# Batch 0 between the two stages of a Fourier mixing kernel: twelve on-chip copies in place of a trip through memory, another order of the first loads, and 60 starting products

## The chip, the cores and the metric

The kernel runs on one core of a Trainium2 chip. A core has a matrix engine (PE in the profile, with its weight loads as PEld), a vector engine (DVE), a scalar engine (ACT), GpSimd (POOL) and SyncE (SP), each with an instruction stream of its own that runs in order and waits on semaphores. SP, ACT and POOL issue transfers, and 16 DMA engines carry them out. SBUF is the on-chip memory of 128 partitions, PSUM the memory into which PE writes. The metric is the time of one execution on the device in microseconds (us), lower is better.

## The reference, cut to what matters

```python
# x: (8, 2496, 256)
X = np.fft.fft(np.fft.fft(x, axis=1), axis=2).real      # mixing over the sequence, then over the features
t = X.reshape(19968, 256)
logits = t @ w_gate                                      # 8 experts
e = argmax(logits, 1)
gate = softmax(logits)[e]
y = relu(t @ w1[e]) @ w2[e]                              # w1[e]: 256 x 1024, w2[e]: 1024 x 256
out = gate * y
```

Each of the 8 sequences ("batches") is transformed as a whole, and every one of its 2496 tokens then goes through one expert. Transforms and expert products are in float32.

## The kernel before, in words

The transform of a batch has two stages. **First stage** (`first`, L325): x of a batch comes in three thirds, `xq` (`load`, L284), each 112 partitions x 2048 floats, 896 KB, in three buffers. DVE folds a third (`fold`, L299; `fold_d`, L292), which uses the symmetry of the transform over positions and over features, and leaves four slices. PE multiplies each slice by a table of waves, `w1` (`half1`, L311), into PSUM tiles `s1`; ACT copies two slices at a time into `t1`. The third's four slices are written to a DRAM tensor `Td` of the batch (L342), and when all three are there, two transfers (`regroup`, L351) read it back as `t4`, in which the partition is another index of the transform: 120 values that belong together lie in 120 partitions, in 11 groups. For batches 0 and 1 ACT issues the writes, for the later ones SP. For each third of batch b > 0 that has been used, `load` asks for a third of batch b + 1.

**Second stage** (`second`, L361). `turn_last` (pr in the profile) mends one column of `t4`; `group` (p, from t and table) does the short transform of a group into `zz`; for each of ten windows of 128 rows PE does the transform over the features and the gate's logits at once (p, from zz and table), ACT copies what is left over, and DVE forms two sets of result rows (L410). After five windows `route` (L416) picks each row's expert and its place in a sorted list `Xs` in DRAM (rk are PE's running counts). Ten scatters per half then send the rows there: POOL issues them (`send`, L462). For batch 0 the places come from DVE as whole numbers; for later batches ACT and POOL turn them.

**Experts** (`experts`, L730). `plan` (L478) makes lists of blocks of 512, 256 or 128 rows of one expert. For each block SP reads an offset from such a list, then the rows (xb, `fetch_rows`) and the weights (w_sb, `fetch_weights`, 2 x 1 MB). DVE turns the rows (xT), PE does the product with w1 (ph), relu follows, PE does the product with w2 (py), and POOL scatters the rows into the output. Batch 0 has two blocks of 256 and four of 128.

**Order.** The order of instructions on each engine is the program's order, written out by hand: generators that are advanced in turns. `ahead_of(b)` (L930) is the first stage and the regrouping; `mixed(b)` (L936) advances the second stage of b together with the first stage of b + 1. The main part loads the constants, issues 16 products of ones (`WARM`), runs the first stage of batch 0 to its end, asks for x of batch 1 and for the regrouped values, prepares the gate's table (pg), takes seven steps of batch 1's first stage, and then runs the second stage of batch 0, with one step of batch 1 at every second step. Then expert work is taken step by step, with side work of the next batches at a rate that comes from the amount of work. Before the first block of all, nine turns of side work are taken (L784) between the request of its rows and the turning of its rows.

Of the kernel before, what the change touches and what calls it, by code (L numbers as in the profile page):

```python
# [12 lines left out]
F32 = mybir.dt.float32  # L13
# [8 lines left out]
NA, NB = 104, 24  # L22
# [10 lines left out]
HALF = -(-NG // 2)  # L33
LAST = NW * 128 - (NG - 1) * GP
NT = B * S
E, F = 8, 1024
# [149 lines left out]
AHEAD = 12  # L186
WARM = 16
MOST = max(k for now in rounds() for _, k, _ in now)
# [27 lines left out]
def kernel(ctx: ExitStack, tc, x, w_gate, w1, w2, out):  # L216
# [64 lines left out]
    ones = cp.tile([128, 128], BF16, name="ones16")  # L281
    waves = const_dram("w1", consts["w1"])

    def load(b, q):  # L284

        if b < B:
            xq = xp.tile([NP, 8, D], F32, tag="xq", name="xq", bufs=3)
            row = (b * NQ + q) * NA
            nc.sync.dma_start(out=xq[:].rearrange("p j d -> p (j d)"), in_=x[row:row + NP])
            ahead[b, q] = xq[0:NA]  # L290

    def fold_d(o, a, n):  # L292
# [30 lines left out]
    ahead = {}  # L323

    def first(b):  # L325

        pm0 = xp.tile([NA, D], F32, tag="pm0", name="pm0")
        for q in range(NQ + 1):
            f = iter(())
            if q < NQ:  # L330
                xq = ahead.pop((b, q))
                f = fold(xq, q, pm0[:])
            next(f, None)
            yield
            if q:
                t1 = xp.tile([NP, 4, D], F32, tag="t1", name="t1")
                half1(b, q - 1, 0, pm, pm0, t1)
            next(f, None)
            yield
            if q:  # L340
                half1(b, q - 1, 1, pm, pm0, t1)
                (nc.sync if b > 1 else act).dma_start(out=Td[b][:, 4 * (q - 1) * D:4 * q * D], in_=t1[:].rearrange("p j d -> p (j d)"))  # L342
                if b:
                    load(b + 1, q - 1)
            next(f, None)
            pm = xq[:, 4:8]
            yield
# [3 lines left out]
    def regroup(b, h):  # L351
        t4 = sp.tile([128, HALF, D], F32, tag="t4", name="t4")
        n = min(HALF, NG - h * HALF)
# [3 lines left out]
        ahead[b, "t4", h] = t4  # L357

    zz = cp.tile([128, 2, NW * 128], F32, name="zz")

# [369 lines left out]
    def experts(todo):  # L730
# [44 lines left out]
        for k, (b, size, last, at) in enumerate(todo):  # L775
            n, m = size // 128, BIG // size
            if not k:
# [5 lines left out]
                fetch_some(0)  # L783
                for _ in range(9):  # L784
                    yield 0, False
# [144 lines left out]
    def ahead_of(b):  # L930

        yield from first(b)
        regroup(b, 0)
        regroup(b, 1)

    def mixed(b):  # L936
# [12 lines left out]
    vec.memset(ones[:], 1.0)  # L949
    act.dma_start(out=con["w1"][:, 0:4], in_=waves[:, 0:4])  # L950
    load(0, 0)
    load(0, 1)
    nc.sync.dma_start(out=con["w1"][:, 4:], in_=waves[:, 4:])
    load(0, 2)
    nc.sync.dma_start(out=table[:], in_=const_dram("table", packed))
    nc.sync.dma_start(out=con["rt"][:], in_=const_dram("rt", consts["rt"]))
    nc.sync.dma_start(out=wg[:], in_=w_gate)
    for k in range(WARM):
# [122 lines left out]
```

## Time and profile before

| what | value |
|---|---|
| median of 3 runs | 1258.53 us (1257.82 to 1259.17) |
| the profiled execution's own time | 1258.56 us |
| its span, first to last instruction | 1256.8 us |
| mean granted PE clock | 0.976 |
| PE busy | 1208.1 us (96%) |
| DVE, ACT, POOL busy | 759.6, 431.3, 447.5 us |
| moved by DMA | 249.79 MB, mean 199 GB/s |
| first product of an expert (ph) starts | 89.55 us |

A row of the profile's timeline gives start and duration in us, engine, line, operation, what is written from what with shapes, the number of instructions in it, and in brackets the idle time of the engine before it and what ended it. In the names buffer numbers are left out, so that w stands for the table of waves, t for t1 and t4, p for the products of the second stage, w_sb for weights. A row of the waits gives the waiting instructions, what they waited for, the total in us, the number of waits and the longest. A row of the chain of work gives start, duration and what ran.

### The profile page before, as it was taken

To read this page: it belongs to the slowest core of one execution; us is meant where nothing else is said; L and a number is where in the kernel's file an instruction comes from. 1 tells how busy PE (TensorE), PEld (TensorE's weight loads), DVE (VectorE), ACT (ScalarE), POOL (GpSimd) and SP (SyncE) were. 2 spreads that over 40 slices of the span, in tenths; PEclk is the share of its full clock that TensorE was granted. 3 is DMA by queue.
4 is the path that set the end of the run, shared out by engine and by line. 5 is a ranking of instruction groups with operands and counts; after the bars stand their busy time and mean duration, and the time that the engine had idled before them with its cause. 6 is when DMAs were issued, how large, how long until landed. Compare 5 with 4: busy or idle time off the path is not lost.

```text
span 1256.8 us, 22295 instructions
## 1 busy us (share of the span) xinstructions
PE 1208.1 (96%) x7289; PEld 1076.3 (86%) x7289; DVE 759.6 (60%) x1804; ACT 431.3 (34%) x1167; POOL 447.5 (36%) x527
## 2 busy tenths in 40 slices
PE   5759999999999999999999999999999999999997
PEld 3648998777788899888988899889999999999996
DVE  3455434343456788566866578686888784444653
ACT  1424332333243433434343333442333332222222
POOL 0154527054117522472226603472364241111112
PEclk6869999999999999999999999999999999999998
DMA  8859899873548434673336435453347237878787
GB/s 235 261 174 350 308 317 311 221 237 122 154 153 263 151 110 163 184 234 116 102 124 211 138 96 162 138 180 101 106 139 206 94 105 284 277 285 284 280 292 284
DMA packets 163216, 249.79 MB, mean 199 GB/s; under 512 B 118601, under 2 KB 130227, under 8 KB 143516
## 3 DMA queue, kind: packets, MB, share of 16 engines
q1 hardware_dynamic: 146327, 203.28, 50.7%
q0 software_dynamic: 15888, 42.14, 9.1%
q10 hardware_dynamic: 885, 2.94, 0.7%
q8 instruction: 59, 0.97, 0.3%
q14 instruction: 57, 0.47, 0.1%
HBM read 194.91 MB, written 54.83 MB: 199 GB/s over the span
## 4 chain that ended last, share of the span: by engine, by line
PE 82%; DVE 9%; DMA 4%; ACT 2%; issue 2%; POOL 0%; SPq 0%; POOLq 0%; DVEq 0%; ACTq 0%
PE py L221 25%; PE ph L221 13%; PE a L221 11%; PE c L221 9%; PE p L221 6%; PE b L221 6%; PE d L221 5%; PE e L221 4%; PE s L221 3%; DMA xq<-in_x_dram 1%; DVE xT L584 1%; DMA Td<-t 1%; DVE y L684 1%; DMA Xs<-rows,pi 1%; DVE hT L639 1%
## 5 line engine op out<-in xcount | busy, mean ns | idle before, releaser
L236 POOL DMA_INDIRECT out_dram<-y,ro x163 | 161.4, 990 | 625.3 <-ACT y L680 301.3
L221 PE MATMUL py<-w_sb,hT 128*128 128x256 f32 x1504 | 339.5, 379 | 0.0
L221 PEld LDWEIGHTS py<-w_sb,hT 128*128 128x128 f32 x1504 | 281.4, 190 | 36.9 <-issue 1.0
L236 POOL DMA_INDIRECT Xs<-rows,pi x160 | 162.4, 1015 | 112.0 <-DVE rows L410 56.7
L221 PE MATMUL ph<-xT,w_sb 128*128 128x128 f32 (+2 forms) x992 | 171.1, 328 | 11.2 <-DVE xT L584 11.1
L221 PEld LDWEIGHTS ph<-xT,w_sb 128*128 128x128 f32 x992 | 136.3, 192 | 35.1 <-issue 16.8
L410 DVE SCALAR_TENSOR_TENSOR rows<-p,zs 128x129 f32<-128x129 f32 x160 | 48.9, 348 | 128.8 <-ACT lg L408 124.8
L221 PE MATMUL a<-xT,w_sb 128*128 128x256 f32 (+1 forms) x512 | 117.8, 357 | 0.0
L838 DVE TENSOR_SCALAR hT<-ph 128x512 f32<-128x512 f32 x43 | 29.7, 691 | 123.7 <-PE ph L221 63.7
L587 ACT ACTIVATE xT<-xT 128x256 f32<-128x256 f32 (+1 forms) x94 | 36.5, 388 | 179.2 <-DVE xT L584 140.8
L221 PEld LDWEIGHTS a<-xT,w_sb 128*128 128x128 f32 x512 | 88.6, 190 | 9.7
L892 ACT ACTIVATE y<-py,xb 128x256 f32<-128x256 f32 x94 | 44.6, 475 | 152.2 <-PE py L221 152.2
L636 DVE TENSOR_TENSOR hT<-hT,b 128x512 f32<-128x512 f32 x57 | 39.2, 688 | 75.7 <-PE b L221 50.0
L646 ACT ACTIVATE hT<-a 128x512 f32<-128x512 f32 x57 | 34.0, 597 | 134.1 <-PE a L221 131.1
L221 PE MATMUL s<-xq,w 104*112 104x256 f32 (+2 forms) x208 | 62.8, 425 | 16.3 <-DVE xq L297 12.1
L469 POOL CAST pi<-due 128x1 int32<-128x1 f32 x140 | 45.1, 322 | 65.5 <-ACT due L468 65.5
L221 PE MATMUL a<-w_sb,hT 128*128 128x128 f32 x528 | 66.0, 276 | 0.0
L221 PEld LDWEIGHTS a<-w_sb,hT 128*128 128x128 f32 x528 | 63.1, 192 | 0.7
L221 PEld LDWEIGHTS p<-table,t 120*128 120x128 f32 x352 | 53.6, 202 | 10.6 <-ACT t L372 2.8
L221 PE MATMUL c<-xT,ws 128*128 128x256 f32 (+1 forms) x256 | 60.3, 362 | 1.0 <-DVE hT L642 0.2
L221 PEld LDWEIGHTS s<-xq,w 104*112 104x112 f32 x208 | 38.5, 204 | 26.3 <-DVE xq L297 10.8
L584 DVE STREAM_TRANSPOSE xT<-xb 128x512 f32<-128x512 f32 (+1 forms) x91 | 56.2, 631 | 7.6 <-DMA xb<-Xs 7.6
(149 smaller groups left out, 2072.6 us busy)
## 6 DMA issues: line engine op xcount, KB each, us to landing
w_sb<-in_moe_w_dram SPq DMA_DIRECT2D x132, 1024.0 KB
xq<-in_x_dram SPq DMA_DIRECT2D x24, 896.0 KB
xb<-Xs SPq DMA_DIRECT2D x112, 128.0 KB
Td<-t SPq DMA_DIRECT2D x18, 448.0 KB
t<-Td SPq DMA_DIRECT2D x8, 768.0 KB
t<-Td SPq DMA_DIRECT2D x8, 640.0 KB
xb<-Xs SPq DMA_DIRECT2D x52, 64.0 KB
xb<-Xs SPq DMA_DIRECT2D x88, 32.0 KB
```

The lines of the kernel that those rows point to most:

```text
L221: nc.tensor.matmul(o, lhsT=lhsT, rhs=rhs, start=start, stop=stop, **kw)
L236: return unordered(pool.indirect_dma_start(out=dst, out_offset=bass.IndirectOffsetOnAxis(ap=idx, axis=0), in_=rows, in_offset=None, bounds ...
L410: vec.scalar_tensor_tensor(rows[:, k + m, 0:NY], p3[:, 0:NY], zs[:, 0:1], zs[:, 1:], op0=ALU.add, op1=op)
L469: pool.tensor_copy(idx, due[:])
L584: vec.transpose(free(xT[:], 256 * h, [32, n // 32], [BIG, 2], [1, 32]), free(xb, 512 * h, [64, n // 32], [1, 2], [2, 32]))
L587: act.activation(odd, odd, ACTF.Copy, scale=-1.0)
L636: vec.tensor_tensor(h12, h11, b[:], op=add)
L639: vec.tensor_tensor(h21, h12, d[:], op=add)
L646: act.activation(h11, a[:], ACTF.Relu)
L684: vec.tensor_tensor(o, o, p[:], op=add)
L838: vec.tensor_scalar(o, ph[:], 0.0, None, op0=ALU.max)
L892: act.activation(y[:, i % 2], py[:], ACTF.Copy, scale=meta[:, i, 1:2])
```

## The change

**Between the stages, batch 0 alone.** `first_whole` takes the place of `first(0)`. It folds and multiplies two slices at a time. Its table of waves, `wp`, has 110 columns in another order, so that after ACT's copy a slice lies in `t1` as 110 partitions, and one transfer inside SBUF per slice (12 in all: even slices by ACT, odd ones by SP) puts it where the second stage reads it: 10 partitions, 12 apart, x 11 groups x 256 floats. Td and the regrouping are not used for batch 0. `t4` is now one tile `t4s` for all batches, in two halves; before, each half came from a pool of two buffers. `natural` makes the table of waves for the other batches, `w1`, from `wp`, with three copies of DVE.

**Order of the first loads.** The waves come in three pieces (slices 0 to 3, 4 to 7, the rest), and the last third of x of batch 0 in two halves. `table`, `rt`, `wg`, the constants `bt` and the pad rows of `Xs` are now issued by POOL, behind a one-element copy that waits for the last piece of waves. x of batch 1 is asked for by SP inside `first_whole`: the first third after the eighth slice's copy, the other two after the twelfth. The last third of x of batch 2 is asked for after batch 1's regrouping.

**Turns.** 60 products of ones in place of 16. Three steps of batch 1's first stage stand before batch 0's second stage in place of seven, and the interleaving begins at the second stage's step 4. Twelve turns of side work stand before the first block in place of nine.

```diff
+NR = 2 * NU * NG
...
-WARM = 16
+WARM = 60
...
-    waves = const_dram("w1", consts["w1"])
+    wp = bp.tile([128, NS + 3, NR], F32, tag="w2", name="wp", bufs=3)[0:NA]
+    order = consts["w1"][:, :, 0:NR].reshape(NA, NS + 3, NG, 2 * NU).swapaxes(2, 3)
+    waves = const_dram("w1", order.reshape(NA, NS + 3, NR))
...
+    def pieces(xq, row):
+            for k in range(2):
+                nc.sync.dma_start(
+                    out=xq[:].rearrange("p (c j) d -> p c j d", c=2)[:, :, 2 * k:2 * k + 2],
+                    in_=x[row:row + NP].rearrange("p (c j d) -> p c j d", c=2, d=D)[:, :, 2 * k:2 * k + 2])
+                yield
...
+    def first_whole():
+        pm0 = xp.tile([NA, D], F32, tag="pm0", name="pm0")
+        for q in range(NQ):
+            xq = ahead.pop((0, q))
+            t1 = xp.tile([NP, 4, D], F32, tag="t1", name="t1")
+            for lo in (0, 2):
+                end = q == NQ - 1 and lo
+                a, m = xq[:, lo:lo + 2], xq[:, 4 + lo:6 + lo]
+                n = 2
+                if end:
+                    n = 1
+                    fold_d(pm0[:], m[:, 1], 1)
+                vec.tensor_tensor(a[:, 0:n], a[:, 0:n], m[:, 0:n], op=ALU.add)
+                fold_d(m, a, 2)
+                ps = pm_.tile([NP, 2, D], F32, tag="m", name="s1")
+                for i in range(2):
+                    s = 4 * q + lo + i
+                    o = ps[0:NR, i]
+                    if s < NS - 1:
+                        mm(o, columns(s), m[:, i])
+                        continue
+                    for k, l, r in ((NS - 1, 0, H + 1), (NS + 1, H + 1, D)):
+                        mm(o[:, l:r], columns(k), pm0[:, l:r], True, False)
+                        mm(o[:, l:r], columns(k + 1), m[:, 1, l:r], False, True)
+                if end:
+                    for i in range(2):
+                        act.copy(t1[0:NR, lo + i], ps[0:NR, i])
+                else:
+                    act.copy(t1[0:NR, lo:lo + 2], ps[0:NR])
+                for i in range(2):
+                    s = 4 * q + lo + i
+                    (nc.sync if s % 2 else act).dma_start(out=t4s[s:GP:NS, 0:NG], in_=t1[0:NR, lo + i])
+            if q:
+                load(1, q - 1)
+        load(1, NQ - 1)
+        for lo in range(0, NS + 3, 5):
+            natural(lo, lo + 5)
+        for h in range(2):
+            ahead[0, "t4", h] = t4s[:, h * HALF:(h + 1) * HALF]
+
+    def columns(s):
+        return wp[:, s]
+
+    def natural(lo, hi):
+        n = hi - lo
+        vec.tensor_copy(free(con["w1"][:, lo:hi], 0, [NP, n], [2 * NU, NG], [1, 2 * NU]),
+                 free(wp[:, lo:hi], 0, [NR, n], [1, NG], [NG, 2 * NU]))
...
-                if b:
+                if b > 1 or b and q < NQ:
                     load(b + 1, q - 1)
...
-        t4 = sp.tile([128, HALF, D], F32, tag="t4", name="t4")
+        t4 = t4s[:, h * HALF:(h + 1) * HALF]
...
-                for _ in range(9):
+                for _ in range(12):
                     yield 0, False
...
         regroup(b, 1)
+        if b == 1:
+            load(b + 1, NQ - 1)
...
-    act.dma_start(out=con["w1"][:, 0:4], in_=waves[:, 0:4])
+    vec.memset(con["w1"][:, :, NR:], 0.0)
+    act.dma_start(out=wp[:, 0:4], in_=waves[:, 0:4])
     load(0, 0)
     load(0, 1)
-    nc.sync.dma_start(out=con["w1"][:, 4:], in_=waves[:, 4:])
-    load(0, 2)
-    nc.sync.dma_start(out=table[:], in_=const_dram("table", packed))
-    nc.sync.dma_start(out=con["rt"][:], in_=const_dram("rt", consts["rt"]))
-    nc.sync.dma_start(out=wg[:], in_=w_gate)
+    nc.sync.dma_start(out=wp[:, 4:8], in_=waves[:, 4:8])
+    rest = load(0, 2, 2)
+    next(rest)
+    nc.sync.dma_start(out=wp[:, 8:], in_=waves[:, 8:])
+    next(rest)
+    came = cp.tile([1, 1], F32, name="came")
+    pool.tensor_copy(came[:], wp[0:1, NS + 2, 0:1])
+    pool.dma_start(out=table[:], in_=const_dram("table", packed))
+    pool.dma_start(out=con["rt"][:], in_=const_dram("rt", consts["rt"]))
+    pool.dma_start(out=wg[:], in_=w_gate)
+    pool.dma_start(out=bt[:], in_=const_dram("blocks", cv))
+    sent(unordered(pool.dma_start(
+        out=Xs[E * CAP:].rearrange("(k p) w -> p k w", k=BLK // 128), in_=bc(pad[:], 1, BLK // 128)), "xs"), 0)
...
-    for _ in first(0):
-        pass
-    load(1, 0)
-    load(1, 1)
-    regroup(0, 0)
-    regroup(0, 1)
-    load(1, 2)
-    nc.sync.dma_start(out=bt[:], in_=const_dram("blocks", cv))
-    sent(unordered(nc.sync.dma_start(
-        out=Xs[E * CAP:].rearrange("(k p) w -> p k w", k=BLK // 128), in_=bc(pad[:], 1, BLK // 128)), "xs"), 0)
+    first_whole()
...
-    for _ in range(7):
+    for _ in range(3):
         next(early)
     for k, _ in enumerate(second(0)):
-        if k % 2 == 0:
+        if k > 3 and k % 2 == 0:
             next(early, None)
```

More of the change, by code (lines that the diff above doesn't have):

```diff
@@ L281, with load @@
     ones = cp.tile([128, 128], BF16, name="ones16")
-    waves = const_dram("w1", consts["w1"])
-    def load(b, q):
+    wp = bp.tile([128, NS + 3, NR], F32, tag="w2", name="wp", bufs=3)[0:NA]
+    order = consts["w1"][:, :, 0:NR].reshape(NA, NS + 3, NG, 2 * NU).swapaxes(2, 3)
+    waves = const_dram("w1", order.reshape(NA, NS + 3, NR))
+    def load(b, q, parts=1):
         if b < B:
@@ L288, in load @@
             row = (b * NQ + q) * NA
-            nc.sync.dma_start(out=xq[:].rearrange("p j d -> p (j d)"), in_=x[row:row + NP])
             ahead[b, q] = xq[0:NA]
+            if parts == 1:
+                nc.sync.dma_start(out=xq[:].rearrange("p j d -> p (j d)"), in_=x[row:row + NP])
+                return iter(())
+            return pieces(xq, row)
+    def pieces(xq, row):
[4 more added lines that the diff above has]
+                yield
     def fold_d(o, a, n):
@@ L357, in regroup @@
         ahead[b, "t4", h] = t4
+    t4s = cp.tile([128, 2 * HALF, D], F32, name="t4s")
     zz = cp.tile([128, 2, NW * 128], F32, name="zz")
```

## The prediction

> **What bounds the kernel now.** I read the page first (busy shares, then the 40 slices of 31.4 us).
>
> ```profile
> span 1256.8 us, 22295 instructions
> PE 1208.1 (96%) x7289; PEld 1076.3 (86%) x7289; DVE 759.6 (60%) x1804; ACT 431.3 (34%) x1167; POOL 447.5 (36%) x527
> ...
> PE   5759999999999999999999999999999999999997
> ...
> PEclk6869999999999999999999999999999999999998
> DMA  8859899873548434673336435453347237878787
> ```
>
> PE is full from the fourth slice on; only the first three have room. The busy time by stages finds its end: from 89.55 to 1256.8 PE is busy 1155.8 of 1167.25 us, so 11.5 us are idle there and 37.2 of the page's 48.7 before. In the rows the columns are the stretch, its length, busy time (and count) of PE, weight loads, DVE, ACT, POOL, the granted clock, DMA share, GB/s.
>
> ```profile
> 60.00:70.00 10.00, 4.45 (x25) 3.79 (x25) 8.91 (x44) 1.56 (x5) 7.87 (x8) 0.61 0.68 239
> 70.00:80.00 10.00, 7.24 (x40) 6.00 (x38) 7.42 (x34) 4.76 (x18) 7.87 (x8) 0.88 0.84 304
> 80.00:90.00 10.00, 0.45 (x1) 0.45 (x2) 1.97 (x6) 0.42 (x1) 2.72 (x3) 0.64 0.29 70
> 90.00:100.00 10.00, 10.00 (x55) 8.52 (x54) 4.21 (x16) 2.90 (x9) 0.00 (x0) 0.85 0.79 245
> ```
>
> So the time is: moment of the first expert product (ph), plus PE work left after it. PE's waits up to there, and the timelines of PE and POOL, name the way to that moment:
>
> ```profile
> PE s L221 <- DVE xq L297: 12.1, 3, 6.3
> PE ph L221 <- DVE xT L584: 11.1, 1, 11.1
> PE rk L221 <- DVE oh L431: 5.1, 2, 3.5
> ```
> ```profile
> 35.83 0.57 PE L221 MATMUL pr<-t,table 120*120 120x6 f32 x2 [1.24 <-DMA t<-Td]
> ...
> 62.68 0.54 PE L221 MATMUL pr<-t,table 120*120 120x6 f32 x2 [0.20 <-DMA t<-Td]
> ...
> 89.55 2.93 PE L221 MATMUL ph<-xT,w_sb 128*128 128x256 f32 x6 [11.06 <-DVE xT L584]
> ```
> ```profile
> 55.19 1.11 POOL L236 DMA_INDIRECT Xs<-rows,pi  x1 [54.73 <-DVE rows L410]
> ...
> 82.36 0.97 POOL L236 DMA_INDIRECT Xs<-rows,pi  x1 [0.30 <-issue]
> ```
>
> Batch 0's second stage starts at 35.83 (first pr), its 20 scatters run back to back on POOL from 55.19 to 83.3, the block is read and turned, ph starts at 89.55: 34.36 us after the first scatter. Batch 1's second stage (pr at 62.68) stands ahead of ph in PE's order. The chain of work shows what made 35.83:
>
> ```profile
> 15.51 10.59 DMA Td<-t
> ...
> 27.27 3.61 DMA Td<-t
> ...
> 32.05 8.97 DMA xq<-in_x_dram
> ...
> 57.11 5.44 DMA t<-Td
> ```
>
> The trip through Td is 27.27 to 35.8, 8.5 us; and the first write (15.51) took 10.6 us beside x of batch 1, which held ACT's third pair of copies until 26.17.
>
> **What the Trainium skill says.** "DMA: Bandwidth & Descriptors", section "Why a DMA increments its semaphore by 16 and not by 1": a DMA uses the largest count of engines up to 16 that divides both slowest dimensions; 10 and 110 give 10 engines for each new copy. No run here shows that yet. Same page, "Anatomy of one DMA — SWDGE (gpsimd) path": a fixed cost of about 2 us (given for GpSimd's DMAs); the read xb<-Xs on the chain took 1.98 us, so the trace agrees. Same page, "Issuing engines are not separate DMA queues": SP's, ACT's and POOL's transfers share the engines; the 10.6 us write agrees. "TensorE: Matmul & The Clock Gate", "Part 1: The HAM clock gate": half clock until about 3.4 us of activity, and again after an idle window. Here 16 products of ones take 3.41 us (213 ns each), 8 ph from 89.55 take 3.66 us and the 8 at 94.00 take 1.89: it agrees.
>
> **The change, part by part.**
>
> *Order of loads.* Table and rt (429 + 256 KB) leave SP's line and go to POOL behind the last waves. The third x of batch 0 landed at 18.89; 0.69 MB at the 231 GB/s of 10 to 20 us is 3.0 us, so 15.9; the first copies join (4 x 110 KB, about half of their 2 us exposed): I take 17.0 (15.5 to 19). POOL gets five DMAs (table, rt, wg, and bt and the pad of Xs, which stood in SP's line before) at about 1 us each to issue (nearest: scatter 0.97), done near 21, where POOL idled until 55.19. If they land later than the copies, pg and pr wait one for one.
>
> *Folding by halves.* A whole fold is 2.64 us (8.41 to 11.05), so the first products can start near 9.9 instead of 11.1. After the last half: pm 0.6, add 0.35, fold 0.85 make 19.0; products 1.3 us at full clock (2.6 at half, half of what 21.82 to 26.4 shows), copies 0.7: 21.0 to 22.3.
>
> *60 products of ones.* 44 more, at 213 ns 9.4 us, at full clock 4.7. They lie in PE's idle stretch 4.75 to 11.1 and end at 9.5 to 11.2 if the clock rises; were it to stay half, at 14.1, which costs up to 2.5 us at the end of the stage. Gain of full clock: up to 1.3 us in the last part. I count nought.
>
> *Twelve copies for the Td trip.* Each moves 110 KB in 1 KB rows; two are left after the last evacuation. No row shows SBUF to SBUF. Lower bound the 2 us fixed; upper: SP's s = 9 and 11 stand in its line behind load(1, 0) (896 KB, 3.3 us by 8.4 to 11.72), on 10 engines, 7 us. I take 2.5. So pr at 24.5 (22.5 to 30) against 35.83: 11.3 us earlier. ACT's extra issues, 4 x 0.31, stand between its copies, hidden by the waits for x. The three copies of waves to natural order (550 elements; 1024 take 1.23, so 0.66 each, 2.0 us of DVE) lie under the copies' landing; uncovered they would cost that 2.0. The old pool held one batch in its two buffers, so the single tile adds no wait.
>
> *pr to first scatter.* Before 19.36 us, with four pairs of batch-1 products in it and 2.7 us of DVE folding in line before the rows. After: pr, turn, two groups and the first window's rows take about 5.1 (half clock); four more windows at 1.16 (rows at 56.37 and 57.53) are 4.6, and the folds of 1.22 and 1.4 among them, a little of them in DVE's own waits, add 2.5; the route is 3.5 (50.69 to 54.2), and 1.5 of the last third's fold stands inside it: 17.2, and 1.0 to POOL: 24.5 + 18.2 = 42.7. Gain 12.5. x of batch 1 is asked for at 17.5, 21 and 21.5, three times 3.3 us behind the table: about 22, 27, 31, each just before its fold; late by 4 us they would cost that much.
>
> *Scatters.* 34.36 us as before: ph no sooner than 77.1.
>
> *Batch 1's line.* Here the change gives back. Of batch 1 only three steps go ahead of batch 0's second stage now, not seven. In the new order all of batch 1's last third (s of q = 2) stands behind the second rk of batch 0. That rk I place at 51 (42 + 9); products 2.5, copy 0.6, Td1 at 54; write 3.3, regroup 4.5 to 5.4: pr of batch 1 near 62, as before (62.68). Then, ahead of ph on PE, stand five windows instead of four and three pairs of s instead of two (turns 9 to 12), and on DVE the route's first seven operations (2.1) and a fold (1.35) ahead of xT. From 62: 2.7 for pr and groups, s 2.0, five windows and the second s near 8, route and fold 3.45, xT 0.71 and 0.42 less overlap on ACT: ph at 79.3 (76.5 to 84). This is later than 77.1 and decides: 10.2 us earlier than 89.55.
>
> *Work done early.* One window (8 p in 0.95) and one pair of s (0.88) no longer lie behind ph: 1.8 us.
>
> Weights are asked for behind regroup and load(2, 2), near 59, and need some 10 us: hidden under the scatters by about 8. From ph on the work on every queue is what it was, with the same loads relative to it; batch 1's scatters ended at 141.2, its first block's read came at 169.02, so 28 us of slack cover a shift.
>
> Sum: 10.2 + 1.8 = 12.0. The profiled execution took 1258.56 (1256.8 span, 1.8 around it), the median 1258.53: 1246.5.
>
> **Rivals.**
>
> *The scatters alone decide* (batch 1's line hides, or the clock stays up because PE's pause before ph shrinks, worth 1.7): ph at 75 to 77, gain 14 to 17.5: 1241 to 1244.5. For it: POOL's unbroken 27 us. Against: the new items ahead of xT.
>
> *Copies or x late*: 10 engines and a line shared with 896 KB put pr at 28 to 32, or x of batch 1 stalls the folds. Gain 3 to 9: 1249.5 to 1255.5. For it: Td<-t needed 10.6 us in just such company.
>
> *Same*: if PE is at bottom fed by batch 1's Td trip, moving batch 0 moves nothing: pr of batch 1 near 72, ph at 89.5, 1256 to 1261. Against: 28 us of slack, and scatters that began at 55.
>
> *Slower*: batch 1's line overtakes. It decides beyond a landing of t<-Td of batch 1 at 74, 12 us later than I place it (two full load waits of 3.3 us, and a Td write of 10.6 like that at 15.51 instead of 3.3, would reach it). Then each us costs one; with 5 more, 1263.
>
> **Numbers.** Forecast (1244.5 to 1249.5) 0.53; scatters alone 0.17; late copies 0.20; same 0.03; slower 0.07. Three runs spread 0.1%; 0.2% (2.5 us) is about what can be told. Faster 0.90, same 0.03, slower 0.07. Range 1240.5 to 1255 leaves about 0.11 out.
>
> **What would show it.** pr of batch 0 near 24.5; first scatter near 43; scatters without breaks; pr of batch 1 near 62; ph near 79 with xT waiting on DVE's queue rather than on xb<-Xs; after ph, PE idle still near 11.5 us. Wrong if the copies take over 7 us, if x of batch 1 holds DVE ahead of rows, or if PE idles between 90 and 160.

## The result, and the profile after

The changed kernel takes 1263.08 us (median of 10 runs, 1261.28 to 1266.12) against 1258.82 us for the kernel before beside it: a ratio of 1.0031, 95% interval 1.0022 to 1.0039. It is slower by 0.3%, where 1246.5 us had been forecast. Run again on two more occasions, on two chips, it gave 1.0020 (1.0006 to 1.0034) and 1.0024 (1.0006 to 1.0042).

The page after; the digits are again the busy tenths of 40 slices.

```profile
span 1262.3 us, 22419 instructions
PE 1213.0 (96%) x7333; PEld 1080.0 (86%) x7333; DVE 763.6 (60%) x1820; ACT 430.8 (34%) x1168; POOL 449.2 (36%) x533
...
PE   6759999999999999999999999999999999999997
...
PEclk8779999999999999999999999999999999999999
DMA  9579999773648434673346435443346238788877
```

The picture is the same: most of what is lost lies in the first three slices. PE's waits up to 100 us (what waits, for what, total, number of waits, longest) have changed places, though:

```profile
PE pr L222 <- DMA t4s<-Td: 10.1, 1, 10.1
PE pr L222 <- DMA t4s<-t: 9.2, 1, 9.2
PE rk L222 <- DVE oh L495: 5.4, 2, 3.3
PE ph L222 <- DVE ro L857: 4.5, 1, 4.5
```

Before, the longest two were for x and, 11.1 us, for the block's rows on their way to ph. Now PE stands twice before a second stage: 9.2 us for the new copies, 10.1 us for batch 1's regrouping. PE's timeline gives the places:

```profile
1.35 11.28 PE L222 MATMUL py<-ones 128*128 128x256 bf16 x60 [1.35 <-DVE warm L1037]
...
34.13 0.54 PE L222 MATMUL pr<-t4s,table 120*120 120x6 f32 x2 [9.19 <-DMA t4s<-t]
...
61.41 0.21 PE L222 MATMUL rk<-oh,tri 128*128 128x88 bf16 x1 [3.34 <-DVE oh L495]
...
75.90 0.54 PE L222 MATMUL pr<-t4s,table 120*120 120x6 f32 x2 [10.08 <-DMA t4s<-Td]
...
93.88 6.42 PE L222 MATMUL ph<-xT,w_sb 128*128 128x256 f32 x16 [4.47 <-DVE ro L857]
```

pr of batch 0 moved from 35.83 only to 34.13. Batch 1's pr, which stood at 62.68, moved to 75.90, and ph from 89.55 to 93.88: 4.33 us later. From ph to the end it is 1168.4 us, 1.2 more than before; 4.3 + 1.2 is the 5.5 by which the span of the profiled execution grew. POOL's scatters, which had set ph before, no longer do: they start sooner and end sooner (51.57 and 79.0, against 55.19 and 83.3), and POOL then stands idle.

```profile
51.57 1.07 POOL L237 DMA_INDIRECT Xs<-rows,pi  x1 [32.64 <-DVE rows L474]
...
78.04 0.97 POOL L237 DMA_INDIRECT Xs<-rows,pi  x1 [0.30 <-issue]
```

The chain of work shows what made 34.13 and 75.90: two of batch 0's copies end to end, and later the write and the regrouping of batch 1.

```profile
17.20 7.89 DMA t4s<-t
25.15 8.41 DMA t4s<-t
...
66.48 3.08 DMA Td<-t
69.68 6.08 DMA t4s<-Td
```

SP's own timeline, then POOL's, show what lay beside these two copies:

```profile
14.19 5.21 SPq L371 DMA_DIRECT2D t4s<-t  x4
19.58 0.96 SPq L294 DMA_DIRECT2D xq<-in_x_dram  x1
22.29 3.62 SPq L371 DMA_DIRECT2D t4s<-t  x2
```
```profile
15.80 0.74 POOL L1027 DMA_DIRECT2D table<-c_table  x1
...
18.14 0.79 POOL L1031 DMA_DIRECT2D Xs<-pad  x1
```

Slices 9 and 11, SP's last two copies, go out behind 896 KB of x of batch 1. The last one is issued only at 25.15, when the fifth copy of all (ACT's, asked for at 17.20) has landed (why it waits for that one the profile does not say), and then needs 8.41 us itself. ACT is held too: its fifth evacuation (its fifth copy out of PSUM) waits 3.06 us for copies to leave `t1`. And there is a second load beside the copies: between 15.80 and 18.93 POOL asks for the constants and the pad rows, 951 KB together, which before the change stood in SP's line.

### The profile page after: what moved, and what is told of

Same layout as the page of the kernel before. It is cut to its first block, busy times and chain, and to the rows that moved or that the text cites. A ratio compares the mean times of both kernels' runs of the same rounds, so it can differ in the third digit from the quotient of the medians.

```text
span 1262.3 us, 22419 instructions
## 1 busy us (share of the span) xinstructions
PE 1213.0 (96%) x7333; PEld 1080.0 (86%) x7333; DVE 763.6 (60%) x1820; ACT 430.8 (34%) x1168; POOL 449.2 (36%) x533
## 4 chain that ended last, share of the span: by engine, by line
PE 85%; DVE 8%; DMA 3%; ACT 2%; issue 2%; SPq 0%; ACTq 0%; POOL 0%; POOLq 0%; DVEq 0%
PE py L222 25%; PE ph L222 13%; PE a L222 11%; PE c L222 10%; PE p L222 7%; PE b L222 6%; PE d L222 5%; PE e L222 4%; PE s L222 4%; DMA t4s<-t 1%; DVE xT L648 1%; DVE y L748 1%; DMA xb<-Xs 1%; DVE hT L700 0%; DVE hT L706 0%
## 5 line engine op out<-in xcount | busy, mean ns | idle before, releaser
L222 PEld LDWEIGHTS p<-table,t4s 120*128 120x128 f32 x352 | 54.7, 205 | 9.0 <-issue 2.6
L222 PE MATMUL p<-table,t4s 120*128 120x120 f32 (+1 forms) x352 | 57.7, 290 | 1.9 <-ACT t4s L436 1.9
L222 PE MATMUL p<-table,zz 128*128 128x145 f32 (+1 forms) x320 | 57.3, 303 | 2.2 <-ACT zz L443 1.3
L222 PE MATMUL b<-xs,ws 128*128 128x256 f32 (+1 forms) x256 | 58.7, 356 | 0.0
```

Source lines behind the costliest of these rows:

```text
L222: nc.tensor.matmul(o, lhsT=lhsT, rhs=rhs, start=start, stop=stop, **kw)
```

## The experiments

The executions were spread over several chips, on which the kernel before took between 1258.8 and 1274.7 us. They stand in six groups (column g); every ratio below is to the runs of before in the same group, and moments are from one profiled execution each. All changes are made to the changed kernel, unless it says "to before". "Rest" is the span from ph to the end.

The kernel before has a profile in group 1 alone, so that moments are best compared inside a group. And ph gives the time only where the rest stays the same. In groups 1 and 4 it does, within 4 us (1166.6 to 1170.4). In the other four it is 1173.2 to 1187.2, and inside each of them it is longer the earlier ph is, so that there an earlier ph is in part paid back. PE idles more in that stretch (from 100 to 160 us it is busy 55.9 us in after2 and 54.3 in a_turns2, against 59.7 in after). Why is not shown.

| run | g | edit | pr batch 0 | first scatter | pr batch 1 | ph | rest | ratio (95%) |
| --- | --- | --- | --- | --- | --- | --- | --- | --- |
| before | 1 |  | 35.83 | 55.19 | 62.68 | 89.55 | 1167.3 | 1 |
| after | 1 |  | 34.13 | 51.57 | 75.90 | 93.88 | 1168.4 | 1.0031 (1.0022-1.0039) |
| after2 | 3 | the changed kernel again | 34.16 | 51.56 | 83.10 | 100.88 | 1175.1 | 1.0020 (1.0006-1.0034) |
| after3 | 5 | the changed kernel again | 32.66 | 51.19 | 82.74 | 99.65 | 1174.7 | 1.0024 (1.0006-1.0042) |
| a_behind | 2 | x behind the copies | 29.73 | 49.46 | 74.17 | 91.31 | 1180.8 | 0.9988 (0.9969-1.0006) |
| b_turns | 2 | to before: new turns | 34.78 | 53.41 | 90.05 | 107.80 | 1173.2 | 1.0036 (1.0018-1.0055) |
| a_turns2 | 3 | old turns, own t4 | 36.01 | 58.35 | 65.49 | 92.52 | 1187.2 | 1.0055 (1.0036-1.0073) |
| a_mid | 3 | seven early steps | 37.06 | 56.30 | 70.57 | 93.39 | 1182.4 | 1.0035 (1.0020-1.0050) |
| a_mid_behind | 3 | seven early steps, and x behind | 38.62 | 56.60 | 72.00 | 95.48 | 1181.2 | 1.0069 (1.0044-1.0093) |
| a_dense | 4 | every step from 5 on | 35.82 | 55.13 | 71.44 | 90.50 | 1170.4 | 1.0010 (1.0001-1.0020) |
| a_dense_behind | 4 | a_dense, and x behind | 27.72 | 46.89 | 60.82 | 81.04 | 1170.4 | 0.9967 (0.9954-0.9980) |
| dense_behind2 | 6 | a_dense_behind again | 28.66 | 47.94 | 63.84 | 85.32 | 1185.9 | 0.9989 (0.9968-1.0010) |
| a_td | 4 | Td trip, no copies | 31.34 | 49.26 | 73.59 | 91.81 | 1169.5 | 0.9994 (0.9985-1.0004) |
| td_dense | 5 | a_td, and dense turns | 31.30 | 50.60 | 68.28 | 88.52 | 1182.4 | 0.9999 (0.9986-1.0012) |
| td_dense_behind | 6 | td_dense, and x behind | 30.40 | 54.39 | 70.84 | 93.18 | 1183.7 | 1.0030 (1.0013-1.0048) |
| a_warm16 | 4 | 16 products of ones | 34.58 | 53.05 | 74.81 | 91.47 | 1166.6 | 1.0006 (0.9997-1.0014) |
| dense_behind_w16 | 5 | a_dense_behind, and 16 products | 25.99 | 46.25 | 61.63 | 83.31 | 1185.6 | 0.9959 (0.9944-0.9974) |
| b_warm60 | 5 | to before: 60 products | 33.99 | 53.34 | 61.87 | 91.87 | 1179.0 | 1.0016 (0.9996-1.0035) |

### Are the copies slow in themselves?

**a_iso**: x of batch 1 and the constants of POOL wait, by a small read of `t4s`, until all twelve copies have landed.

```diff
+        nc.sync.dma_start(out=seen, in_=t4s[0:GP, 0:NG, 0])
+        for q in range(NQ):
+            load(1, q)
+        pool.tensor_copy(came[:], t4s[0:1, 0, 0:1])
+        pool.dma_start(out=seen2, in_=t4s[0:GP, 0:NG, 1])
+        constants()
```

> The changed kernel with SP and POOL made to wait for all twelve copies (by a small read of what they wrote) before x of batch 1 and before table, rt, wg, bt and the pad: the copies run beside nothing but x of batch 0. Only the landing of the copies is read from it, the time not (x and table are late on purpose). Theory 'queueing': the small read is issued within 3 us of the last evacuation (about 21), at 23 to 25. Rival 'slow in themselves': at 28 or later.

SP's timeline, then ACT's, and the chain of work of that run:

```profile
14.07 8.46 SPq L373 DMA_DIRECT2D t4s<-t  x6
25.01 0.89 SPq L374 DMA_DIRECT2D seen<-t4s  x1
```
```profile
19.66 0.59 ACT L370 COPY t<-s 110x512 f32<-110x512 f32 x1 [1.16 <-DMA t4s<-t]
...
21.51 0.79 ACTq L373 DMA_DIRECT2D t4s<-t  x1
```
```profile
15.64 3.87 DMA t4s<-t
...
21.78 3.11 DMA t4s<-t
```

SP's sixth copy is out at 22.53 and the read of `t4s` at 25.01, so by then all twelve have landed. That is 3.3 us after the last evacuation (21.75), a little beyond the 3 us expected and far from the rival's 28. From its issue to its landing a copy takes 3.1 to 3.9 us here, beside its own kind alone, where the changed kernel shows 7.9 and 8.4. ACT waits 1.16 for copies in place of 3.06, and SP needs 8.46 us for its six in place of going on until 25.9. So the copies are not slow in themselves: the 2.5 us of the prediction, counted from the last evacuation, would have been 3.3. What cost is the company. (The time of this run, 1296 us, means nothing, since x and the constants are late on purpose.)

**a_behind**: only x of batch 1 goes behind the copies.

```diff
-            if q:
-                load(1, q - 1)
-        load(1, NQ - 1)
+        for q in range(NQ):
+            load(1, q)
```

> The changed kernel with all three requests for x of batch 1 behind the twelve copies on SP, in place of the first one ahead of the last two odd copies. Theory 'queueing': the copies' packets are short and wait behind x, so the last copies land by 26 to 29 and pr of batch 0 starts at 27 to 30 (34.1 in the changed kernel); ph is then earlier by the same 4 to 7 us: 1256 to 1260. Rival 'slow in themselves' (10 engines, 1 KB rows, table beside them): pr at 32 to 35, 1262 to 1266.

pr of batch 0 comes at 29.73 in place of 34.13, as PE's timeline of this run has it. The profile names nothing that released it:

```profile
24.21 1.00 PE L222 MATMUL pg<-wg,rt 128*128 128x8 f32 x4 [3.95 <-DMA wg<-in_moe_w_gate_dram]
...
29.73 0.54 PE L222 MATMUL pr<-t4s,table 120*120 120x6 f32 x2 [3.17 <-issue]
```

So x of batch 1 beside the last copies costs 4.4 us at pr. But the first copies are as slow as they were. ACT's and SP's timelines and the chain of work of a_behind:

```profile
24.02 0.58 ACT L368 COPY t<-s 110x512 f32<-110x512 f32 x1 [5.41 <-DMA t4s<-t]
```
```profile
27.07 1.42 SPq L294 DMA_DIRECT2D xq<-in_x_dram  x3
```
```profile
15.76 8.12 DMA t4s<-t
```

ACT's fifth evacuation waits 5.41 us for a copy that takes 8.12, and x of batch 1 is not asked for before 27.07. What lies beside this copy are POOL's constants; a_iso holds them back too, and there the same copy takes 3.87 (6.03 and 7.18 in a_dense_behind and dense_behind2, which have x behind and the constants beside). The packets of the three traces say the same. From 16 to 21 us, before the first packet of x of batch 1 in each of them, the copies move 447 KB in the changed kernel and 380 in a_behind, beside 768 and 668 KB of constants, and 820 KB in a_iso beside none.

The first loss so has two causes, both shown. The constants hold the first copies up and with them the last evacuation (23.77 in the changed kernel, 26.11 in a_behind, 21.75 in a_iso). x of batch 1 then makes it 10.4 us from the last evacuation to pr, in place of 3.6. With x alone moved, 4.4 us are won; with the constants moved as well, all copies have landed by 25.01, another 4.7 us ahead of that pr.

But batch 1's pr comes at 74.17, hardly sooner than 75.90. x of batch 1 is now later itself: DVE begins its first fold at 34.21 (29.89 in the changed kernel), and this fold stands ahead of batch 0's first rows. So the first scatter is only 2.1 us earlier and the second rk 1.1.

**a_td** puts the trip back and keeps the rest of the change.

```diff
-                    (nc.sync if s % 2 else act).dma_start(out=t4s[s:GP:NS, 0:NG], in_=t1[0:NR, lo + i])
+            act.dma_start(out=Td[0][:, 4 * q * D:4 * (q + 1) * D], in_=t1[:].rearrange("p j d -> p (j d)"))
+            if q == 1:
+                load(1, 0)
+        regroup(0, 0)
+        regroup(0, 1)
+        load(1, 1)
+        load(1, 2)
```

> The changed kernel with the trip through Td for batch 0 put back (three writes by ACT, the regrouping on SP ahead of the second and last third of x of batch 1), everything else of the change kept: order of loads, folds by halves, 60 products of ones, turns. Theory 'the copies, held up in their queues, are no quicker than the trip they replace': pr of batch 0 at 31 to 35 (34 with the copies), ratio within 0.001 of the changed kernel's. Rival 'the copies bring some microseconds even so': pr of batch 0 at 37 or later.

The chain of work of a_td:

```profile
22.81 3.49 DMA Td<-t
26.35 4.86 DMA t4s<-Td
31.34 0.54 PE pr L222 x2
```

The trip takes 8.5 us from the last evacuation, as before the change, and reaches pr 2.8 us sooner than the copies do. In the order that the change gives them the copies are a loss, where the two had been expected within 0.001: 0.9994 (0.9985 to 1.0004) here against 1.0020 to 1.0031 for the changed kernel. These stand in other groups, but none of its three intervals meets this one.

### The turns

**b_turns** does the new turns alone on the kernel before.

```diff
-                for _ in range(9):
+                for _ in range(12):
...
-    for _ in range(7):
+    for _ in range(3):
...
-        if k % 2 == 0:
+        if k > 3 and k % 2 == 0:
```

> The kernel before with the turns of the changed one alone (three steps, interleaving from step 4, twelve turns). Theory 'batch 1's line': the second rk stays near 60 to 62, batch 1's last third comes behind it, its pr near 72 to 76, ph at 90 to 94, less 1.8 us of work done early: 1259.5 to 1263, slower than before by 1 to 4. Rival: the turns do nothing or help, because batch 0's rows no longer stand behind batch 1's folds: 1252 to 1258.

It is slower by as much as the whole change. The profile forbids to put all of that down to the late products, though. SP's and ACT's timelines and the chain of work of b_turns:

```profile
47.18 29.48 SPq L289 DMA_DIRECT2D xq<-in_x_dram  x3
85.08 0.97 SPq L354 DMA_DIRECT2D t<-Td  x2
```
```profile
76.35 0.59 ACT L321 COPY t<-s 112x512 f32<-112x512 f32 x1 [10.05 <-remote]
```
```profile
76.96 8.03 DMA Td<-t
```

The last third's products end at 65.8 by the trace, but ACT's second copy of them waits 10.05 us, for an event that the profile does not name ("remote"). Then the write to Td takes 8.03 us, where it takes 3.08 in the changed kernel, and the regrouping waits for it. Here the last third of x of batch 2 stands ahead of the regrouping in SP's line and goes out just ahead of that write; the change asks for it behind the regrouping. That the write is slow because of this x is likely and was not tried alone, and the 10 us stay unexplained. So b_turns does not size the turns.

**a_turns** is the reverse, the old turns in the changed kernel.

> The changed kernel with the turns of before (seven steps of batch 1 ahead of batch 0's second stage, interleaving from its first step, nine turns ahead of the first block). Theory 'batch 1's line': the first expert product (ph, 93.9 in the changed kernel) waits for batch 1's second stage, whose start (75.9) moved by 13 us because its last third stands behind the second rk of batch 0. Then here pr of batch 1 comes back to 60 to 66, ph follows the scatters (first one + 34.4) at 85 to 89, and the time is 1255 to 1260. Rival 'lost after ph' or 'lost to the copies alone': the turns don't matter, ph stays at 92 to 95, 1261 to 1265.

It gave 1.0112 (1.0077 to 1.0147) and does not test what it was made for: with one tile `t4s`, batch 1's regrouping comes ahead of batch 0's last reads in this order, so the last groups of batch 0 are computed of batch 1's values and the work behind them differs. With the single tile, batch 1's regrouping has to stand behind batch 0's last read, and this asks for late turns. **a_turns2** therefore gives batch 1 and the later ones their two buffers back.

```diff
-        t4 = t4s[:, h * HALF:(h + 1) * HALF]
+        t4 = sp.tile([128, HALF, D], F32, tag="t4", name="t4")
...
-    t4s = cp.tile([128, 2 * HALF, D], F32, name="t4s")
+    t4s = bp.tile([128, 2 * HALF, D], F32, tag="hT", name="t4s", bufs=1)
```

> The changed kernel with the turns of the kernel before (seven early steps, one at every second step from the start, nine turns before the first block). So that batch 1's values need not wait for batch 0's last reads, batch 1 and the later ones get the two pool buffers of before again; t4s serves batch 0 alone and lies in the space of hT, which is first written at ph. Theory 'the new turns hold batch 1 back': the last third's products of batch 1 stand ahead of the second rk again, pr of batch 1 comes at 62 to 66 in place of 76, ph at 85 to 87 (first scatter + 34), and the time is 0.3 to 0.6% below the kernel before. Rival 'the copies alone cost it': pr of batch 0 stays near 34, nothing is regained, ratio 1.002 or more. Rival 'the turns are paid back after ph': ph is early but the idle of PE after ph grows by as much, ratio 0.999 to 1.002.

Half of it held. Batch 1's pr is at 65.49, as the theory said (62 to 66): the turns do hold batch 1 back. But ph is at 92.52, not 85 to 87. Nor is the kernel faster: beside the changed kernel in the same group (after2) ph is 8.4 us earlier, the rest 12.1 us longer, and the ratio 1.0055 against 1.0020. So here the earlier ph was paid back behind it, as the last of the rivals had it, and by more. PE's and POOL's timelines of a_turns2:

```profile
65.49 0.35 PE L222 MATMUL pr<-t,table 120*120 120x6 f32 x2
...
92.52 3.78 PE L222 MATMUL ph<-xT,w_sb 128*128 128x256 f32 x8 [4.59 <-DVE xT L648]
```
```profile
58.35 1.07 POOL L237 DMA_INDIRECT Xs<-rows,pi  x1 [39.86 <-DVE rows L474]
```

As to ph, the first scatter has moved to 58.35, 6.8 us later than in the changed kernel, and 58.35 + 34.2 is ph. With seven early steps, two pairs of batch 1's products stand ahead of pr of batch 0 in PE's order and wait for x of batch 1, and its folds stand ahead of batch 0's rows on DVE. **a_mid** and **a_mid_behind** (seven early steps, the interleaving from step 4) say the same.

> The changed kernel with its single t4s, but seven early steps in place of three (the interleaving still begins at step 4) and nine turns before the first block in place of twelve. The last third's products of batch 1 then stand two windows ahead of the second rk, and its regrouping behind the last read of batch 0's t4s. Theory 'the new turns hold batch 1 back': products at 55 to 58 in place of 61.7 to 65.8, pr of batch 1 near 68, ph near 86, 0.2 to 0.6% below the kernel before. Rival 'the copies alone cost it': ratio 1.002 or more.

> As a_mid, and all three thirds of x of batch 1 are asked for behind the twelve copies. If late copies and late turns are the two separate causes, this has the sum: pr of batch 0 near 30, first scatter near 48 to 50, pr of batch 1 near 67, ph near 84, 0.4 to 0.8% below the kernel before. If the late copies did not matter once batch 1's line is short, it equals a_mid within 0.1%.

First scatters are at 56.30 and 56.60, ph at 93.39 and 95.48, and both are slower than before. x behind the copies seems to make it worse here (the two intervals just meet), and PE waits longer for x ahead of pr (38.62). In these two the scatters do not run unbroken either: POOL stops for 3.42 and 5.14 us ahead of the second ten, which stand behind the second rk (69.05 and 71.52). So two lines meet at ph: batch 0's scatters (first scatter plus about 34 us, more where they break), and batch 1's own line (with twelve turns its pr plus about 17). Early steps lengthen the first, late turns the second.

**a_dense** takes the three early steps, and then a step of batch 1 at every step of batch 0's second stage from the sixth on, so that the last third's products stand ahead of the second rk and the regrouping still behind batch 0's last read. **a_dense_behind** has x behind the copies as well.

```diff
-                for _ in range(12):
+                for _ in range(9):
...
-        if k > 3 and k % 2 == 0:
+        if k > 4:
```

> The changed kernel with three early steps as it has them, but from step 5 of batch 0's second stage on a step of batch 1 at every step, not every second, and nine turns before the first block. So batch 0's rows of the first half stay early, and batch 1's last third stands ahead of the second rk. Theory 'two lines meet at ph, batch 0's scatters and batch 1's own; three early steps shorten the first, the late turns lengthen the second': first scatter near 52 as in the changed kernel (seven early steps: 56.3), last third's products near 58 to 61, pr of batch 1 near 70, ph near 86 to 88, ratio to the kernel before 0.997 to 1.000. Rival 'ph early is paid back later': ph near 87 and ratio 1.002 or more.

> As a_dense, with x of batch 1 asked for behind the twelve copies: pr of batch 0 near 30, first scatter near 50, ph near 85 to 87, ratio 0.995 to 0.999. Rival: x of batch 1 is then late for its folds, the last third's products come no sooner than 60, ph at 88 or later and no gain over a_dense.

a_dense misses its first scatter (55.13, not 52): pr of batch 0 was late here too, at 35.82, behind x. With that removed, both lines shorten at once. PE's timeline of a_dense_behind:

```profile
27.72 0.54 PE L222 MATMUL pr<-t4s,table 120*120 120x6 f32 x2 [3.19 <-issue]
...
49.39 0.60 PE L222 MATMUL s<-xq,w 104*112 104x256 f32 x2
...
60.82 0.54 PE L222 MATMUL pr<-t4s,table 120*120 120x6 f32 x2 [4.15 <-DMA t4s<-Td]
...
81.04 3.78 PE L222 MATMUL ph<-xT,w_sb 128*128 128x256 f32 x8 [8.52 <-DVE xT L647]
```

The last third's products end at 50.9 in place of 65.8, batch 1's pr is at 60.82, and ph follows the scatters again (46.89 + 34.2). It is 0.3% faster than before there, and 6.1 us faster than a_dense in the same group; the two intervals do not meet, so in this order x behind the copies is worth 0.4 to 0.5%. Measured once more in group 6 (**dense_behind2**, below) it is 0.9989, above the 0.995 to 0.998 expected, with an interval that holds 1.

### Copies or trip, in the better order

> No copies: batch 0 goes through Td as in a_td, with the turns of a_dense (a step of batch 1 at every step from 5 on, nine turns before the first block). Theory 'the order of turns and of x gives the gain, the copies give only what they save at pr': pr of batch 0 at 31.3 as in a_td, first scatter near 50.5, ph near 85, ratio 0.997 to 1.000, that is 2 to 4 us behind a_dense_behind (pr at 27.7, 0.9967). Rival 'the copies are worth nothing even there': ratio 0.9967 or less.

> The trip through Td, x of batch 1 wholly behind its regrouping, turns of a_dense. Theory 'the copies save what they save at pr': pr of batch 0 at 29 to 31, ph 2 to 4 us later than in the run with copies beside it, ratio 0.002 to 0.004 above it. Rival 'the order of x and turns is all': the two within 0.001 of each other.

> a_dense_behind once more, beside the trip with the same order. Both: pr of batch 0 near 28, ratio to the kernel before 0.995 to 0.998.

td_dense keeps the trip and takes the dense turns: 0.9999, no gain. td_dense_behind and dense_behind2 stood beside one another: 1278.75 and 1273.58 us, so with x behind and the same turns the copies are worth 5.2 us. The two intervals (1.0013 to 1.0048 and 0.9968 to 1.0010) do not touch. The trip is better off with x ahead, however (td_dense), and against that the copies' two measurements gain 0.3% and 0.1%, the second within the intervals. pr of batch 0 differs by only 1.7 us, but the first scatter by 6.5 (54.39 and 47.94). DVE's timeline says why, first of td_dense_behind, then of dense_behind2:

```profile
36.00 1.23 DVE L319 TENSOR_TENSOR xq<-xq 104x1024 f32<-104x1024 f32 x1 [10.41 <-DMA xq<-in_x_dram]
...
38.54 0.61 DVE L469 SCALAR_TENSOR_TENSOR rows<-p,zs 128x129 f32<-128x129 f32 x2
```
```profile
31.75 1.23 DVE L320 TENSOR_TENSOR xq<-xq 104x1024 f32<-104x1024 f32 x1 [5.89 <-DMA xq<-in_x_dram]
...
34.28 0.61 DVE L473 SCALAR_TENSOR_TENSOR rows<-p,zs 128x129 f32<-128x129 f32 x2
```

Batch 1's first fold stands ahead of batch 0's first rows in DVE's order. Behind the trip, x of batch 1 shares the engines with the regrouping and lands at 36.0, 4.25 us later than behind the copies, and the rows wait for its fold. So the copies gain less through pr than by being out of the way when x is asked for. That x lands sooner there is shown; that the regrouping's traffic is what delays it is the likeliest reading, and was not tried alone.

### The 60 products of ones

Each is one constant: `WARM = 16` in the changed kernel (a_warm16), in a_dense_behind (dense_behind_w16), and 60 in the kernel before (b_warm60).

> The changed kernel with 16 products of ones, as before. If the 44 added ones are hidden and only lift the clock early: first s at 9.9 to 10.2 in place of 12.46, but products of the first stage at half clock, the last s ends within 1.5 us of 20.56, pr of batch 0 within 1 us of 34, and no difference in time that can be measured. Rival: the 60 products delay the whole first stage by 2.5 us, and with 16 pr comes 2 us sooner.

> a_dense_behind with 16 products of ones in place of 60. Theory 'the 60 products hold the first products of batch 0 up to 12.5 and nothing is won back': pr of batch 0 0 to 2 us sooner than 27.7, ph near 79 to 81, ratio 0.994 to 0.997. Rival 'the raised clock is needed': the last products of batch 0's first stage end over 1 us later, ratio 0.997 to 0.999.

> The kernel before with 60 products of ones in place of 16, nothing else. If they are hidden: first s near 12 in place of 11.1, but the last third of x (18.89) sets the end of the stage, so pr of batch 0 stays within 0.5 us of 35.8 and the ratio is 0.999 to 1.001. Rival 'they cost by themselves': first Td write later by 1 us or more, pr at 37 or later, ratio 1.001 to 1.003.

PE's timelines, first of a_warm16, then of the changed kernel:

```profile
9.41 6.10 PE L222 MATMUL s<-xq,wp 104*110 104x256 f32 x16 [4.47 <-DVE xq L311]
```
```profile
12.46 3.67 PE L222 MATMUL s<-xq,wp 104*110 104x256 f32 x16
```

With 16, the first stage begins 3 us sooner, and its first 16 products of waves take 6.10 us, where with 60 they take 3.67 (in the kernel before, 8 such products took 3.75 at a granted clock of 0.50). So its end (20.41, against 20.56) and pr of batch 0 (34.58) are the same within half a microsecond: in this order the 60 products give back what they take. With x behind the copies they do not: there pr comes at 25.99 with 16, at 27.72 and 28.66 with 60. The ratios all point one way (1.0006 against 1.0020 to 1.0031; 0.9959 against 0.9967 and 0.9989; 1.0016 for 60 in the kernel before) but each stands in another group or has an interval that reaches the other, so a cost of 0.1 to 0.2% is likely and not shown. dense_behind_w16, at 0.9959 (0.9944 to 0.9974), has the lowest ratio measured; in its group the changed kernel (after3) has 1.0024 (1.0006 to 1.0042).

### The changed kernel again

> The changed kernel once more, beside the three that follow, so that they share their runs of the kernel before. All theories: the ratio to the kernel before is what it was, 1.002 to 1.004, with pr of batch 0 near 34, the second rk near 61, pr of batch 1 near 76 and ph near 94.

> The changed kernel, so that it stands beside the others of this call. All theories: ratio to the kernel before 1.002 to 1.004, ph near 94.

The ratios are in the range expected. Batch 1's pr is not (83 in place of 76), and ph comes at about 100 in place of 94. Its write and its regrouping took no longer (2.94 and 6.24 us in after3). What came late are ACT's copies of batch 1's last third, as ACT's timeline of after3 has it:

```profile
66.81 0.59 ACT L335 COPY t<-s 112x512 f32<-112x512 f32 x1 [7.46 <-remote]
72.57 0.59 ACT L335 COPY t<-s 112x512 f32<-112x512 f32 x1 [5.17 <-remote]
```

PE's products end at 63.3 by the trace, and what the copies then wait for is not named, as in b_turns. The 7 us do not show in the time.

## Why the prediction was wrong

The frame held for this pair: the time is ph plus PE's work after it. Predicted 79.3 + 1165.45 + 1.8 around the span; measured 93.88 + 1168.4 + 1.8. ph is 14.6 us too early in it, the rest 3.0.

**Order of loads, folding**: the moments were right. DVE starts on the last third at 16.94 (17.0 predicted) and PE ends the stage at 20.56; ACT's last copy ends at 23.8, 1.5 over the range, since it waited for copies to leave `t1` and each issue took 0.79 us, not the 0.31 of the Td write that I had used.

**Twelve copies**: this is the step that failed, at "I take 2.5". From the last evacuation to pr it was 10.4 us (23.77 to 34.13), beyond even the bound of 7 that had been set and that was named among the things that would make the forecast wrong. Together with the late evacuation it put pr 9.6 us later than the 24.5 of the sum. a_iso shows that 3.3 us hold without company, so the operation was priced nearly right and what ran beside it wrongly. The prediction had half of this: the 10.6 us of a Td write "in just such company", and x of batch 1 in SP's line ahead of the last two copies. It counted the bytes ahead of those two, and not that x would slow every copy in flight, nor that the twelfth's issue waits on the fifth. What it took for nothing is the other load, the constants that the change itself moves to POOL: it asked only whether they would land late, and a_behind and a_iso show that they slow the first copies from 3.9 us to 6.0 and up to 8.1. The statement of the Trainium skill used there, that issuing engines are not separate queues ("DMA: Bandwidth & Descriptors", "Issuing engines are not separate DMA queues"), applied to the copies as much as to the Td write: ACT's copy of 17.20 had only copies ahead of it on ACT and took 7.89 us beside what POOL and SP had asked for.

**pr to first scatter**: 17.4, predicted 18.2; **scatters** unbroken, as predicted. So this line would have given a ph at 85.8 (51.57 + 34.2), had it decided.

**Batch 1's line**: the mechanism was right, and it decided as forecast. It had been seen that only three steps go ahead and that the last third stands behind the second rk, and pr of batch 1 was put at 62 for an rk at 51. Each term of it, predicted and measured: rk after pr of batch 0, 26.5 and 27.3; from rk to pr of batch 1, 11 and 14.5 (products 4.1 at a granted clock of 0.58 where 2.5 was taken, write 3.1, regroup 6.1); from there to ph 17.3 and 18.0. So the working of this line fell short by 5 us; 9.6 of the 14.6 are the copies' delay passed on. Before the change the last third's products (49.2 to 50.7), their write and the regrouping ran under batch 0's second half, and pr of batch 1 came 0.7 us after the second rk; now 14.5 us stand between the two. By the measured terms, and with the copies as forecast, ph would have been at 24.5 + 27.3 + 14.5 + 18.0 = 84.3, an estimate: some 5 us ahead of before, not 10. So the copies made the sign, and batch 1's line halved what was there to win.

**Work done early**, 1.8 us: not seen. 12 fewer products lie behind ph (7031 against 7043), and PE is busy there for 1155.5 us against 1155.8. The 16 first ph take 6.42 us where before 8 took 3.66 at half clock and the next 8 took 1.89, 0.9 more; the rest is not explained, and of the size by which single executions differ (1257.82 to 1259.17 before).

**The rival that happened** is "slower: batch 1's line overtakes", with its 0.07. Its threshold (a landing at 74) was passed at 75.8; the causes it had named, a full load wait and a slow write, were not the ones: batch 1's write took 3.1 us. "Copies or x late" came nearer: it named the copies, the line shared with 896 KB and the slow Td write. It put pr at 32 at the latest, and the 5 us that the rest of batch 1's line was short and the 3 after ph are not in it.

## What to carry to other kernels

A transfer that replaces another inherits its company: price it by the row that ran beside the same loads, and before its own size write down every transfer that will be in flight with it, whichever engine asks for it, those that the change itself moves there above all; then what is ahead of it in its queue, and which earlier transfer its issue waits for. When an interleaving is shifted to make room for one line, write out the second line with its own start and end, and ask whether it now hangs on the moment that the first line is late; put the second line's last step ahead of the wait, not behind. A change of several parts may lose as a whole and hold a gain: here copies, x behind them and denser turns together measured 0.1 to 0.4% under the kernel before (in two of three measurements by more than the interval; the lowest is with 16 products of ones), while the copies with x ahead, or the dense turns with the trip, bring nothing. And a moment is not the time: on two chips an earlier ph was in part paid back behind it.

## What was not expected of the hardware

A copy of 110 KB inside SBUF takes 3.1 to 3.9 us from issue to landing beside other copies alone (a_iso), 6.0 to 8.1 us beside 951 KB of constants (a_dense_behind, dense_behind2, a_behind), and 8.4 us beside 896 KB loads of x (the changed kernel). The single packets of a copy (1 KB) hardly show it. In the changed kernel they took 46 ns in the median until 24 us and about 87 from then on, beside x (8 KB, about 530 ns each); 110 packets of 46 ns are 5.1 us of engine time, and several engines share them. By this estimate most of a copy's 8 us lies between its packets, while those of others run.

Each copy ended with ten packets of 4 bytes where a Td write ended with sixteen (60 on ACT's queue for its six copies in the changed kernel, 48 for the three writes of a_td). This fits the ten engines that the prediction worked out; the packet counts are all that shows it.

The issue of such a copy occupies ACT for 0.79 us and SP for 0.77 us, where a Td write occupies ACT for 0.31 us.
